# Seven products for eight in the first feed-forward half from the third block on

## The chip, the cores and the metric

The kernel runs on one NeuronCore of one Trainium2 chip. The metric is the device time of one launch in microseconds (us), lower is better. Matrix products run on TensorE (PE), element-wise work on VectorE (DVE) and ScalarE (ACT), a little on GpSimd (POOL), and all DMAs are issued from SyncE's queue (SP).

## The reference, cut to what matters

Batch 8, sequence 576, model width 512; so 4608 tokens. Chunked attention (8 heads of 64, chunks of 64 tokens) gives x; a layer norm and a feed-forward network (FFN) of width 2048 with residual follow; then a gated convolution and a last projection. float32 throughout.

```python
attn = softmax(q_c @ k_c.T / 8) @ v_c              # per chunk and head
xn = (x - mu) / sqrt(var + 1e-6) * g_ln
ch = maximum(xn @ w_ch1, 0) @ w_ch2                # 512 -> 2048 -> 512
x = x + ch
gate = sigmoid(causal_conv5(x, conv_w));  val = x @ w_val
out = (gate * val) @ w_out
```

## The kernel before

The tokens are cut into nine blocks of 512. Activations lie transposed, features on the partitions, tokens along the row. To keep float32 accuracy with the fast matmul type, every operand is split into a high part (rounded to fp32r) and a low part (the rest), and each product is three matmuls: high by high, high by low, low by high.

For each block b, `unit` (four per block, one per 128 tokens) does the attention, the norm and the transposes, and leaves `xn_t[b]` (high and low part) and `X[b]` (the residual). These rooms alternate between two buffers by b % 2. `ffn(b, f)` does one of 16 steps of the FFN: `one` (lines 672 to 674) multiplies the 128 hidden features of step f by four feature groups kk, 4 x 3 matmuls of 512 columns into a PSUM bank h0 or h1; ACT takes hh (relu, high part, line 680), DVE takes hl (low part, line 684); `two` (lines 695 to 697) adds 4 x 3 matmuls of 512 columns into the four PSUM banks y of the block. `residual` (line 705) adds y to X; `conv(b)` does the convolution of the block and stores X and the convolved rows to DRAM. After the last block the gated stage (`prepare`, `val`, `proj`) loads them again.

The weights of the FFN are loaded and split in block 0 (`weights`, `piece`) and stay: W{g}_{i}, g = 0 to 3 for each quarter of the hidden features, i = 0 to 3 for w_ch1 and 4 to 7 for w_ch2, each a room of 128 x 1024 words. When the last block has used them, the rooms take the weights and tiles of the gated stage.

The order of each engine is fixed when the program is built: `Plan` holds operations with an engine, a duration that the author wrote down, dependences and a due time `pri`, and a list scheduler plays them through; each engine's instructions then stand in that order, and wait by semaphores. `when[b, f]` is the due time of a step.

Of the kernel before, what the change touches and what calls it, by code (L numbers as in the profile page):

```python
# [106 lines left out]
def chunk_attention_ffn_gated_conv(  # L107
# [46 lines left out]

    const = ctx.enter_context(tc.tile_pool(name="const", bufs=1))
# [216 lines left out]
    }  # L372
    X, xn_t, xn_ops, X_ops, evict_ops = {}, {}, {}, {}, {}

    def unit(u):
# [178 lines left out]
        xt = f"xn{b % 2}"  # L554
# [13 lines left out]

        def high():
            if o == 0:  # L570
                xn_t[b] = slot(xt, [P, KD, 2, TB, P], F32R, f"xnt{b}")
            nc.scalar.activation(  # L572
                out=xn_t[b][:, :, 0, o],
                in_=st["ps"][:, 1].rearrange("p (f x) -> p f x", x=P),
                func=AF.Copy,
            )

        def low():
            nc.vector.tensor_tensor(  # L579
                out=xn_t[b][:, :, 1, o],  # L580
                in0=st["ps"][:, 1].rearrange("p (f x) -> p f x", x=P),
                in1=xn_t[b][:, :, 0, o].bitcast(F32),
                op=ALU.subtract,
            )
# [30 lines left out]
        eh = op("ACT", 600, high, tn, take(xt) if o == 0 else xn_ops[b][0][0])  # L615
        el = op("DVE", 700, low, eh)
# [38 lines left out]
    nf, yp, y_ops = [0], {}, {}  # L655

    def ffn(b, f):
# [7 lines left out]
        def one(kk):  # L665
            def go():
# [4 lines left out]
                xh, xl = (xn_t[b][:, kk, s].rearrange("p t x -> p (t x)") for s in range(2))  # L671
# [29 lines left out]
        def residual(p):  # L701
            def go():
                for lo, hi, c in parts(b)[1]:
                    x = X[b][:, 2 * p : 2 * p + 2, c : c + hi - lo]
                    nc.vector.tensor_tensor(out=x, in0=yp[b, p][:, :, lo:hi], in1=x, op=ALU.add)

            return go

        xs = [o for both in xn_ops[b] for o in both]
        o1 = None  # L710
        for kk in range(KD):
            o1 = add("PE", 3 * 230.0, one(kk), xs + [w_op[g, kk], o1] + take(ht), pri)
        oh = add("ACT", 620, high, [o1] + take(hht), pri - 1e8)
# [3 lines left out]
        for p in range(2):  # L717
# [5 lines left out]
            if closes:  # L723
                r = add("DVE", 1300, residual(p), [o2[-1]] + X_ops[b] + y_ops.get((b, p), []), pri - 1e8)
# [4 lines left out]
        if b == NBLK - 1:  # L729
            hold(f"W{g}_{KD + f % 4}", *o2)  # L730
            if f % 4 == 3:
                for kk in range(KD):
                    hold(f"W{g}_{kk}", o1)
        if f == KF - 1:
            hold(f"xn{b % 2}", o1)

# [71 lines left out]
    GROUP = 12 * 230.0  # L808
    xg, x2hl, gvhl, wv, wo = {}, {}, {}, {}, {}
# [34 lines left out]
    def val(j, fo):  # L844
# [112 lines left out]
    for b, f in fstep:  # L957
# [3 lines left out]
        ffn(b, f)  # L961
# [55 lines left out]
```

## Time and profile before

| | |
|---|---|
| time, median of 3 runs (lowest to highest) | 1170.92 us (1170.62 to 1171.21) |
| profiled execution, its own time | 1170.97 us |
| span of that execution on the core | 1169.1 us |
| PE busy | 1142.3 us, 98% |
| weight loads (PEld) busy | 909.0 us, 78% |
| DVE busy | 616.2 us, 53% |
| ACT busy | 361.2 us, 31% |
| DMA | 108.67 MB, mean 93 GB/s |

The span is the time from the first to the last instruction of the core; what lies around it is 1.9 us. PE's busy time counts each matmul with its way through the array, so consecutive matmuls overlap and a busy PE says only that one was always under way. PEld are the loads of the stationary operand, which run beside the matmuls. The first 58 us are attention and weights of block 0; the blocks' FFNs run to 964 us, the gated stage to the end.

### The profile page before, as it was taken

What the parts mean: (1) busy time and instruction counts of PE and PEld (TensorE: products, weight loads), DVE (VectorE), ACT (ScalarE), POOL (GpSimd) and SP (SyncE); (2) the same over time, 40 slices, a digit from 0 to 9 for tenths busy, and PEclk for the clock granted to TensorE, in tenths of its full rate; (3) what the DMA queues carried; (4) which work ended last, traced back from release to release, by engine and by line L of the source; (5) the groups of instructions that cost most, each with busy time, mean ns of one, the idle gap of its engine ahead of it and who ended that gap; (6) DMA issues with size and microseconds to landing.
All of it is one profiled execution on the core that took longest, in us unless ns stands there. A gap on an engine that the chain in (4) does not pass through costs nothing.

```text
span 1169.1 us, 17660 instructions
## 1 busy us (share of the span) xinstructions
PE 1142.3 (98%) x7145; PEld 909.0 (78%) x7145; DVE 616.2 (53%) x1058; ACT 361.2 (31%) x625; POOL 26.2 (2%) x78
## 2 busy tenths in 40 slices
PE   5699999999999999999999999999999999999998
PEld 4477887887778788878878877888788877888886
DVE  5889966337354633744563384455337638334321
ACT  5885522212222221222121122221114524434412
POOL 0000000000000000000000000000000000000000
PEclk9789999999999999999999999999999999999999
DMA  8951233122221321222232132223006306434411
GB/s 204 336 191 28 52 103 100 41 51 88 66 73 54 100 50 41 89 66 72 64 91 50 41 98 66 68 67 89 13 1 224 136 1 208 153 127 151 145 46 72
DMA packets 124938, 108.67 MB, mean 93 GB/s; under 512 B 67508, under 2 KB 108472, under 8 KB 124856
## 3 DMA queue, kind: packets, MB, share of 16 engines
q1 hardware_dynamic: 124856, 107.54, 30.9%
q8 instruction: 56, 0.92, 0.3%
q14 instruction: 26, 0.21, 0.1%
HBM read 79.19 MB, written 28.31 MB: 92 GB/s over the span
## 4 chain that ended last, share of the span: by engine, by line
PE 94%; DVE 2%; SPq 1%; DMA 1%; ACT 1%; issue 0%; ACTq 0%; DVEq 0%
PE h L672 12%; PE h L674 12%; PE h L673 12%; PE y L695 12%; PE y L697 11%; PE y L696 11%; PE att L452 4%; PE att L479 3%; PE o L915 3%; PE o L913 3%; PE o L914 3%; PE val L858 3%; PE val L860 3%; PE val L859 3%; PE lo L292 1%; DMA xg<-xgd 1%
## 5 line engine op out<-in xcount | busy, mean ns | idle before, releaser
L672 PE MATMUL h<-xnt,w 128*128 128x512 f32 x576 | 237.0, 411 | 1.4 <-ACT xnt L572 1.4
L684 DVE SCALAR_TENSOR_TENSOR hl<-h,hh 128x512 fp32r<-128x512 f32 x144 | 99.2, 689 | 251.8 <-ACT hh L680 251.8
L695 PE MATMUL y<-hh,w 128*128 128x512 f32 x576 | 231.0, 401 | 0.7 <-ACT hh L680 0.7
L673 PE MATMUL h<-xnt,w 128*128 128x512 f32 x576 | 228.2, 396 | 0.8 <-DVE xnt L579 0.8
L674 PE MATMUL h<-xnt,w 128*128 128x512 f32 x576 | 228.4, 397 | 0.0
L697 PE MATMUL y<-hl,w 128*128 128x512 f32 x576 | 227.4, 395 | 0.0
L696 PE MATMUL y<-hh,w 128*128 128x512 f32 x576 | 226.6, 393 | 0.0
L680 ACT ACTIVATE hh<-h 128x512 fp32r<-128x512 f32 x144 | 86.1, 598 | 436.2 <-PE h L674 430.7
L672 PEld LDWEIGHTS h<-xnt,w 128*128 128x128 f32 x576 | 108.8, 189 | 27.7 <-ACT xnt L572 1.8
L674 PEld LDWEIGHTS h<-xnt,w 128*128 128x128 f32 x576 | 108.8, 189 | 26.0
L697 PEld LDWEIGHTS y<-hl,w 128*128 128x128 f32 x576 | 108.1, 188 | 25.6 <-DVE hl L684 0.4
L695 PEld LDWEIGHTS y<-hh,w 128*128 128x128 f32 x576 | 108.3, 188 | 24.5 <-ACT hh L680 1.1
L673 PEld LDWEIGHTS h<-xnt,w 128*128 128x128 f32 x576 | 109.0, 189 | 23.5 <-DVE xnt L579 1.3
L696 PEld LDWEIGHTS y<-hh,w 128*128 128x128 f32 x576 | 108.3, 188 | 23.5
L777 DVE SCALAR_TENSOR_TENSOR acc<-X,cw_sb,acc 128x516 f32<-128x516 f32 (+1 forms) x144 | 107.4, 751 | 3.3
L864 DVE TENSOR_TENSOR gv<-val,xg 128x512 f32<-128x512 f32 x36 | 24.7, 688 | 70.9 <-PE val L860 70.9
L579 DVE TENSOR_TENSOR xnt<-att,xnt 128x512 fp32r<-128x512 f32 x36 | 24.9, 691 | 66.3 <-ACT X L563 66.3
L858 PE MATMUL val<-x2hl,w 128*128 128x512 f32 x144 | 57.0, 396 | 0.3 <-DVE gv L864 0.3
L860 PE MATMUL val<-x2hl,w 128*128 128x512 f32 x144 | 56.9, 395 | 0.0
L915 PE MATMUL o<-w,gvs 128*128 128x512 f32 x144 | 56.9, 395 | 0.0
L859 PE MATMUL val<-x2hl,w 128*128 128x512 f32 x144 | 56.8, 394 | 0.0
L913 PE MATMUL o<-w,gvs 128*128 128x512 f32 x144 | 56.7, 394 | 0.0
(101 smaller groups left out, 1196.7 us busy)
## 6 DMA issues: line engine op xcount, KB each, us to landing
xg<-xgd SPq DMA_DIRECT2D x36, 512.0 KB, 4.7
raw<-in_moe_w_ch_dram SPq DMA_DIRECT2D x32, 512.0 KB, 8.9
qk_room<-in_q_dram SPq DMA_DIRECT2D x100, 112.0 KB, 2.5
qk_room<-in_k_dram SPq DMA_DIRECT2D x100, 112.0 KB, 2.7
v<-in_v_dram SPq DMA_DIRECT2D x144, 64.0 KB, 2.4
out_dram<-os SPq DMA_DIRECT2D x36, 256.0 KB, 2.0
xgd<-X SPq DMA_DIRECT2D x2, 1024.0 KB, 5.1
xgd<-acc SPq DMA_DIRECT2D x8, 256.0 KB, 2.5
```

The costliest lines, as they stand in the source:

```text
L672: nc.tensor.matmul(ps, wh, xh, start=(kk == 0), stop=False)
L673: nc.tensor.matmul(ps, wh, xl, start=False, stop=False)
L674: nc.tensor.matmul(ps, wl, xh, start=False, stop=(kk == KD - 1))
L684: nc.vector.scalar_tensor_tensor(out=hl, in0=st["ps"], scalar=0.0, in1=st["hh"].bitcast(F32), op0=ALU.max, op1=ALU.subtract)
L695: nc.tensor.matmul(ps, wh[:, s], st["hh"], start=opens, stop=False)
L696: nc.tensor.matmul(ps, wl[:, s], st["hh"], start=False, stop=False)
L697: nc.tensor.matmul(ps, wh[:, s], st["hl"], start=False, stop=closes)
L777: nc.vector.scalar_tensor_tensor(out=a, in0=X[b][:, f, i : i + L], scalar=cw_sb[:, i, f : f + 1], in1=a, op0=ALU.mult, op1=ALU.add,)
L858: nc.tensor.matmul(ps, wh, xh, start=(kk == 0), stop=False)
L859: nc.tensor.matmul(ps, wh, xl, start=False, stop=False)
L860: nc.tensor.matmul(ps, wl, xh, start=False, stop=(kk == KD - 1))
L915: nc.tensor.matmul(ps, al, wh, start=False, stop=(kk == KD - 1))
```

## The change

In blocks 0 and 1 the FFN stays as it was. From block 2 on (`SB = 2`) the first half, hidden = w_ch1.T @ xn, is done per quarter g of the hidden features (512 features by 512 tokens, 512 deep) as a 2 x 2 block product by Strassen's scheme in Winograd's form: seven products of 256 x 256 x 256 in place of eight. Each product is 12 matmuls of 256 columns (two feature groups, two depths, three parts). In detail:

- `weight_sums(g)`, during block 1: forms the four sums of w_ch1's quadrants on DVE (six `whole` steps of two 128x256 adds, four `mix` steps), splits them into high and low parts (ACT, DVE), and stores these and the three plain quadrants to DRAM, 28 pieces `a{g}_{m}` of 512 KB. The rooms W{g}_0 to W{g}_3 are then free.
- Nine of these sixteen rooms become a ring: each product of each block loads its piece from DRAM into the next room of the ring. Six others hold the hidden activations h (three pairs, high and low), one holds an operand.
- `unit` leaves the normalised activations of these blocks unsplit (`xs`); `operands(b)` forms on DVE the four sums of their quadrants and splits the seven operands. They live in block 1's and block 0's former rooms and in W3_3 (`late_tile`).
- `hidden(b, g)`: products 2, 1, 6, 5, 3, 7, 4 in two PSUM banks that are reused within the group. ACT copies of a bank (`shot`) and DVE additions (`join`, `last_join`) make the four quadrants of the hidden activations; relu and split follow as before; the second half is 48 matmuls of 512 columns as before.
- Rooms of the gated stage move, because the ring holds theirs longer. The due times take 21 x 234 ns a step from block 2 on.

The diff, cut to its core:

```diff
+    SB = 2
...
-        t_end += 24 * 230.0
-    ends = {b: when[b, KF - 1] + 24 * 230.0 for b in range(NBLK)}
+        t_end += 24 * 230.0 if b < SB else 21 * 234.0
...
+    ROOMS = [f"W{g}_{i}" for g in range(NG) for i in range(KD)]
+    RING, PAIRS = ROOMS[:9], [ROOMS[9 + 2 * i : 11 + 2 * i] for i in range(3)]
+
+    def late_tile(i):
+        if i not in late:
+            tag, n = ((f"xn{SB % 2}b", 2), (f"xn{1 - SB % 2}a", KD), ("W3_3", 1))[i]
+            late[i] = slot(tag, [P, n, 2 * DM], F32R, f"late{i}")
+        return late[i]
...
+            eh = el = op("ACT", 600, plain, tn, xn_room)
...
+    def weight_sums(g):
...
+        def keep(m, mh, kh):
+            def go():
+                for i in range(2):
+                    for s, t in enumerate(part(mh, 2 * kh + i)):
+                        nc.sync.dma_start(out=a_dram[g, m][:, s, i].bitcast(F32), in_=t)
+
+            a_store[g, m] = add("SP", 2000, go, ready, pri + 5000.0)
+            reads.append(a_store[g, m])
...
+        def whole(ut, m, kh):
+            def go():
+                us[ut] = slot(ut, [P, XW], F32, f"as{g}_{m}{kh}")[:, : 4 * P].rearrange("p (k x) -> p k x", k=2)
+                for i in range(2):
+                    hi, lo = part(m, 2 * kh + i)
+                    nc.vector.tensor_tensor(out=us[ut][:, i], in0=hi, in1=lo, op=ALU.add)
+
+            o = add("DVE", 840, go, ready + take(ut), pri)
...
+        def split(m, ut, i, dep):
+            rt = f"o{'21'[i]}"
...
+            oh = add("ACT", 620, high, [dep] + take(rt), pri)
+            ol = add("DVE", 700, low, [oh], pri)
+            a_store[g, m] = add("SP", 1300, store, [ol], pri)
+            hold(rt, a_store[g, m])
...
+        a = whole("u0", 1, 0)
+        b = whole("u1", 1, 1)
+        s1 = mix("u0", "u0", "u1", ALU.add, a, b)
+        l1 = split("5", "u0", 0, s1)
+        hold("u1", s1)
+        c = whole("u1", 0, 0)
+        s2 = mix("u1", "u0", "u1", ALU.subtract, s1, c)
...
+            hold(f"W{g}_{kk}", last_use[g, kk], *reads)
...
+    def operands(b):
...
+        s2 = split("2", q21, *done)
+        s1 = split("1", q11, *done)
+        t1 = mix(q11, q12, q11, s1)
+        s3 = split("3", q22, *done)
+        t3 = mix(q12, q22, q12, t1)
+        t2 = mix(q22, q22, q11, s3, t3)
+        t4 = mix(q21, q22, q21, s2, t2)
+        last = [split("6", q22, t2, t4), split("5", q11, t1, t2), split("7", q12, t3), split("4", q21, t4)]
+        hold("xs", *last)
...
+        def product(m, into, new, deps):
+            rt = RING[ring_n[0] % len(RING)]
+            ring_n[0] += 1
...
+                x = operand(m)
+                for f in range(2):
+                    for kk in range(2):
+                        wh, wl = (w[m][:, s, kk, f * P : (f + 1) * P] for s in range(2))
+                        for i, (l, r) in enumerate(((wh, 0), (wh, 1), (wl, 0))):
+                            nc.tensor.matmul(
+                                st[into][:, f],
+                                l,
+                                x[:, r, kk],
+                                start=new and f == kk == i == 0,
+                                stop=kk == 1 and i == 2,
+                                skip_group_check=True,
...
+            at = pri + 1400.0 * MS.index(m)
+            ld = add("SP", 1300, load, [a_store[g, m]] + take(rt), at - 16000.0)
+            o = add("PE", 12 * 119.0, go, [ld, B_op[b, m]] + deps, at)
+            hold(rt, o)
...
+        m2 = product("2", "b", True, take(tb))
+        m1 = product("1", "a", True, take(ta))
+        s1 = shot("a", "hh0", m1)
+        c11 = join("hh0", "b", ALU.add, s1, m2)
+        m6 = product("6", "a", False, [m1, s1])
+        m5 = product("5", "b", True, [c11])
+        u2 = shot("a", "hh1", m6)
+        s5 = shot("b", "hl0", m5)
+        m3 = product("3", "b", False, [m5, s5])
+        m7 = product("7", "a", False, [m6, u2])
+        c12 = join("hh1", "b", ALU.add, u2, m3)
+        u3 = shot("a", "hl1", m7)
+        hold(ta, u3)
+        c22 = join("hl0", "hl1", ALU.add, s5, u3)
+        m4 = product("4", "b", True, [c12])
...
+        c21 = add("DVE", 700, last_join, [c22, m4], pri - 1e7)
+        hold(tb, c21)
+
+        hs, h_ops = {}, {}
+        for p, half, tag, dep in ((0, 0, "hh0", c11), (0, 1, "hh1", c12), (1, 1, "hl0", c22), (1, 0, "hl1", c21)):
...
+    XG = [f"W{g}_{i}" for g, lo in ((0, 0), (2, KD)) for i in range(lo, lo + KD)]
+    X2 = [f"W{g}_{i}" for g in (1, 2) for i in range(KD)]
```

The order that the scheduler makes of it, at three places. First TensorE in the middle of block 2. Before, a first-half step (h from xnt and the weights w) and a second-half step (y from hh and hl) of 12 matmuls each alternate:

```order
L695 MATMUL y_1_0_2623<-hh_1_2655,w_520 128x512
L696 MATMUL y_1_0_2623<-hh_1_2655,w_520 128x512
L697 MATMUL y_1_0_2623<-hl_1_2665,w_520 128x512
L695 MATMUL y_1_0_2623<-hh_1_2655,w_520 128x512
L696 MATMUL y_1_0_2623<-hh_1_2655,w_520 128x512
L697 MATMUL y_1_0_2623<-hl_1_2665,w_520 128x512
L452 MATMUL att_2637<-ident,p_2674 128x128 x4
L672 MATMUL h_2_2657<-xnt_1952,w_403 128x512
L673 MATMUL h_2_2657<-xnt_1952,w_403 128x512
L674 MATMUL h_2_2657<-xnt_1952,w_403 128x512
L672 MATMUL h_3_2703<-xnt_1952,w_169 128x512
```

Now products of 256 columns (m from an operand `late` and a loaded piece a) stand between halves of second-half steps; att are the attention's matmuls:

```order
L1044 MATMUL yB_3076<-h_1_1_3281,w_844 128x512
L950 MATMUL m_2_2_3435<-late_2810,a_2_5_3122 128x256 x12
L503 MATMUL att_3448<-kT_3287,qT_3270 64x64 x16
L1042 MATMUL yA_3059<-h_1_1_3280,w_872 128x512
L1043 MATMUL yA_3059<-h_1_1_3280,w_872 128x512
L1044 MATMUL yA_3059<-h_1_1_3281,w_872 128x512
L1042 MATMUL yA_3059<-h_1_1_3280,w_872 128x512
L1043 MATMUL yA_3059<-h_1_1_3280,w_872 128x512
L1044 MATMUL yA_3059<-h_1_1_3281,w_872 128x512
L950 MATMUL m_2_2_3435<-late_2810,a_2_3_3154 128x256 x12
L476 MATMUL att_3448<-ident,p_3472 128x128 x4
```

Each product follows on 6 to 12 matmuls of the second half or on attention work; the number of second-half matmuls has not changed. Second, TensorE at the border of blocks 1 and 2. Before, the first h of block 2 stands ahead of block 1's last y:

```order
L672 MATMUL h_0_2558<-xnt_1952,w_325 128x512
L673 MATMUL h_0_2558<-xnt_1952,w_325 128x512
L674 MATMUL h_0_2558<-xnt_1952,w_325 128x512
L695 MATMUL y_0_0_1760<-hh_15_2562,w_1581 128x512
L696 MATMUL y_0_0_1760<-hh_15_2562,w_1581 128x512
L697 MATMUL y_0_0_1760<-hl_15_2567,w_1581 128x512
L695 MATMUL y_0_0_1760<-hh_15_2562,w_1581 128x512
L696 MATMUL y_0_0_1760<-hh_15_2562,w_1581 128x512
L697 MATMUL y_0_0_1760<-hl_15_2567,w_1581 128x512
L695 MATMUL y_1_0_1771<-hh_15_2562,w_1581 128x512
L696 MATMUL y_1_0_1771<-hh_15_2562,w_1581 128x512
L697 MATMUL y_1_0_1771<-hl_15_2567,w_1581 128x512
```

Now the products of block 2, all but the first, stand behind block 1's last y, one behind the other:

```order
L747 MATMUL y_1_0_1856<-hh_15_2807,w_1666 128x512
L748 MATMUL y_1_0_1856<-hh_15_2807,w_1666 128x512
L749 MATMUL y_1_0_1856<-hl_15_2812,w_1666 128x512
L476 MATMUL att_2790<-ident,p_2829 128x128 x4
L503 MATMUL att_2790<-v_2775,p_2829 64x65 x16
L950 MATMUL m_2_0_2894<-late_2068,a_0_1_2186 128x256 x12
L950 MATMUL m_2_0_2894<-late_2810,a_0_6_2211 128x256 x12
L950 MATMUL m_2_0_2944<-late_2810,a_0_5_2222 128x256 x12
L950 MATMUL m_2_0_2894<-late_2810,a_0_7_2319 128x256 x12
L950 MATMUL m_2_0_2944<-late_2810,a_0_3_2302 128x256 x12
L950 MATMUL m_2_1_3009<-late_2068,a_1_2_2405 128x256 x12
L950 MATMUL m_2_0_3031<-late_2919,a_0_4_2372 128x256 x12
```

What stood on both sides of the border is now on one side. Third, DVE in block 1, from one low part of hidden activations (hl_2) to the next (hl_3 and hl_4). Before:

```order
L684 SCALAR_TENSOR_TENSOR hl_2_1879<-h_2_1822,hh_2_1865 128x512
L777 SCALAR_TENSOR_TENSOR acc_3_1844<-X_389,cw_sb,acc_3_1844 128x512 x3
L524 TENSOR_SCALAR rs_1900<-att_1781 128x8
L525 RECIPROCAL rs_1900<-rs_1900 128x8
L527 TENSOR_TENSOR x_1903<-att_1781,rs_1900 128x2x4x64
L535 BN_STATS stat_1905<-x_1903 128x6
L537 BN_AGGR mv_1906<-stat_1905 128x2
L538 TENSOR_SCALAR ve_1908<-mv_1906 128x1
L684 SCALAR_TENSOR_TENSOR hl_3_1929<-h_3_1867,hh_3_1922 128x512
L546 TENSOR_SCALAR xn_1934<-x_1903,mv_1906,rstd_1924 128x512
L579 TENSOR_TENSOR xnt_1952<-att_1781,xnt_1952 128x4x128
L684 SCALAR_TENSOR_TENSOR hl_4_1993<-h_4_1918,hh_4_1987 128x512
```

Now with the sums of weights (as):

```order
L736 SCALAR_TENSOR_TENSOR hl_2_1964<-h_2_1907,hh_2_1950 128x512
L1098 SCALAR_TENSOR_TENSOR acc_3_1929<-X_419,cw_sb,acc_3_1929 128x512 x3
L823 TENSOR_TENSOR as_10_1985<-w_197 128x256
L823 TENSOR_TENSOR as_10_1985<-w_248 128x256
L548 TENSOR_SCALAR rs_1991<-att_1866 128x8
L549 RECIPROCAL rs_1991<-rs_1991 128x8
L551 TENSOR_TENSOR x_1994<-att_1866,rs_1991 128x2x4x64
L559 BN_STATS stat_1996<-x_1994 128x6
L561 BN_AGGR mv_1997<-stat_1996 128x2
L562 TENSOR_SCALAR ve_1999<-mv_1997 128x1
L736 SCALAR_TENSOR_TENSOR hl_3_2015<-h_3_1952,hh_3_2010 128x512
L570 TENSOR_SCALAR xn_2025<-x_1994,mv_1997,rstd_2017 128x512
```

Sums stand between hl_2 and hl_3; behind hl_4 the next sums follow at once.

## Rows read from the trace of the kernel before

**Rows 1.** The page: engines; granted TensorE clock in 40 slices; chain that ended last.

```profile
PE 1142.3 (98%) x7145; PEld 909.0 (78%) x7145; DVE 616.2 (53%) x1058; ACT 361.2 (31%) x625; POOL 26.2 (2%) x78
...
PEclk9789999999999999999999999999999999999999
...
PE 94%; DVE 2%; SPq 1%; DMA 1%; ACT 1%; issue 0%; ACTq 0%; DVEq 0%
```

**Rows 2.** Windows: 0 to 100 us, the gated stage, then blocks 1 and 2.

```profile
core 0: us, PE busy (x) PEld busy (x) DVE busy (x) ACT busy (x) POOL busy (x), PEclk, DMA share, GB/s
0.00:100.00 100.00, 78.01 (x594) 56.34 (x595) 78.76 (x156) 70.64 (x128) 5.16 (x17) 0.90 0.72 214
...
1000.00:1100.00 100.00, 100.00 (x432) 80.78 (x431) 34.96 (x54) 39.12 (x69) 0.00 (x0) 1.00 0.43 138
...
166.30:264.50 98.20, 98.20 (x677) 78.56 (x676) 48.65 (x83) 20.80 (x35) 2.64 (x8) 1.00 0.25 71
264.50:365.50 101.00, 101.00 (x689) 80.82 (x689) 50.92 (x86) 21.46 (x37) 2.64 (x8) 1.00 0.25 68
```

**Rows 3.** Groups by line and shape on TensorE: second half, transposes, loads (mean ns).

```profile
L674 PE MATMUL h<-xnt,w 128*128 128x512 f32 x576 | 228.4, 397 | 0.0
...
L674 PEld LDWEIGHTS h<-xnt,w 128*128 128x128 f32 x576 | 108.8, 189 | 26.0
...
L452 PE MATMUL att<-ident,p 128*128 128x128 f32 x144 | 22.2, 277 | 1.6 <-ACT p L508 1.6
...
L452 PEld LDWEIGHTS att<-ident,p 128*128 128x128 f32 x144 | 17.9, 141 | 6.3 <-ACT p L508 1.9
```

**Rows 4.** Timeline of TensorE about 502 us: start, duration, engine, line.

```profile
502.02 0.39 PE L697 MATMUL y<-hl,w 128*128 128x512 f32 x1
...
502.26 0.60 PE L452 MATMUL att<-ident,p 128*128 128x128 f32 x4
502.58 0.19 PEld L672 LDWEIGHTS h<-xnt,w 128*128 128x128 f32 x1
502.61 0.48 PE L672 MATMUL h<-xnt,w 128*128 128x512 f32 x1
502.69 0.19 PEld L673 LDWEIGHTS h<-xnt,w 128*128 128x128 f32 x1
502.93 0.40 PE L673 MATMUL h<-xnt,w 128*128 128x512 f32 x1
```

**Rows 5.** Groups by line and shape on DVE and ACT (mean ns).

```profile
L684 DVE SCALAR_TENSOR_TENSOR hl<-h,hh 128x512 fp32r<-128x512 f32 x144 | 99.2, 689 | 251.8 <-ACT hh L680 251.8
L680 ACT ACTIVATE hh<-h 128x512 fp32r<-128x512 f32 x144 | 86.1, 598 | 436.2 <-PE h L674 430.7 <-DVE X L705 4.9
...
L427 DVE STREAM_TRANSPOSE qT<-qk_room 128x512 f32<-128x512 f32 x28 | 30.8, 1101 | 0.0
...
L500 DVE TENSOR_TENSOR p<-att,mx 128x512 f32<-128x512 f32 x36 | 24.9, 692 | 1.2
...
L579 DVE TENSOR_TENSOR xnt<-att,xnt 128x512 fp32r<-128x512 f32 x36 | 24.9, 691 | 66.3 <-ACT X L563 66.3
...
L499 DVE TENSOR_REDUCE mx<-att 128x8 f32<-128x512 f32 x36 | 24.6, 683 | 4.2 <-PE att L479 4.1
...
L572 ACT ACTIVATE xnt<-att 128x512 fp32r<-128x512 f32 x36 | 21.5, 597 | 68.2 <-PE att L452 68.1
...
L705 DVE TENSOR_TENSOR X<-y,X 128x896 f32<-128x896 f32 x4 | 4.3, 1086 | 2.3 <-PE y L697 2.2
...
L563 ACT ACTIVATE X<-att 128x256 f32<-128x256 f32 x8 | 2.6, 386 | 0.0
...
L705 DVE TENSOR_TENSOR X<-y,X 128x256 f32<-128x256 f32 x4 | 1.7, 420 | 2.2 <-PE y L697 2.1
...
L705 DVE TENSOR_TENSOR X<-y,X 128x128 f32<-128x128 f32 x4 | 1.1, 287 | 2.3 <-PE y L697 2.2
```

**Rows 6.** DMA issues by line: count, KB each, median us to landing.

```profile
xg<-xgd SPq DMA_DIRECT2D x36, 512.0 KB, 4.7
raw<-in_moe_w_ch_dram SPq DMA_DIRECT2D x32, 512.0 KB, 8.9
```

More of the change, by code (lines that the diff above doesn't have):

```diff
@@ L653, in weights, with residual @@
         )
-    nf, yp, y_ops = [0], {}, {}
+    nf, yp, y_ops, last_use = [0], {}, {}, {}
+    def residual(b, p):
+        def go():
+            for lo, hi, c in parts(b)[1]:
+                x = X[b][:, 2 * p : 2 * p + 2, c : c + hi - lo]
+                nc.vector.tensor_tensor(out=x, in0=yp[b, p][:, :, lo:hi], in1=x, op=ALU.add)
+        return go
     def ffn(b, f):
@@ L723, in ffn @@
             if closes:
[L724 removed]
+                r = add("DVE", 1300, residual(b, p), [o2[-1]] + X_ops[b] + y_ops.get((b, p), []), pri - 1e8)
                 y_ops[b, p] = [r]
@@ L728, in ffn @@
         hold(hlt, *o2)
[L729 to L733, printed above, removed]
         if f == KF - 1:
             hold(f"xn{b % 2}", o1)
+    MS = ("2", "1", "6", "5", "3", "7", "4")
+    WA = dict(zip(MS, ("12", "11", "S2", "S1", "S4", "S3", "22")))
+    a_dram = {
+        (g, m): dram.tile([P, 2, 2, 2 * P], F32R, name=f"a{g}_{m}") for g in range(NG) for m in MS
+    }
@@ new lines, in chunk_attention_ffn_gated_conv, with quadrant, mix, go @@
+    B_op = {}
+    def operands(b):
+        pri = when[b, 0] - 12000.0
+        done = [o for both in xn_ops[b] for o in both]
+        if b == SB:
+            for m in "6537":
+                hold(f"o{m}", *take(f"xn{1 - SB % 2}"))
+            hold("o4", *take("W3_3"))
+        def quadrant(kh, h):
+            return xn_t[b][:, 2 * kh : 2 * kh + 2, h * 2 * P : (h + 1) * 2 * P]
+        def mix(to, x, y, *deps):
+            def go():
+                nc.vector.tensor_tensor(out=quadrant(*to), in0=quadrant(*x), in1=quadrant(*y), op=ALU.subtract)
+            return add("DVE", 700, go, deps, pri)
+        def split(m, src, *deps):
+            def high():
+                nc.scalar.activation(out=operand(m)[:, 0], in_=quadrant(*src), func=AF.Copy)
+            def low():
+                t = operand(m)
+                nc.vector.tensor_tensor(
+                    out=t[:, 1], in0=quadrant(*src), in1=t[:, 0].bitcast(F32), op=ALU.subtract
+                )
+            oh = add("ACT", 620, high, list(deps) + take(f"o{m}"), pri)
+            B_op[b, m] = ol = add("DVE", 700, low, [oh], pri)
+            return ol
+        q11, q12, q21, q22 = ((kh, h) for kh in range(2) for h in range(2))
+        s2 = split("2", q21, *done)
[7 more added lines that the diff above has]
+        hold("xs", *last)
@@ L960, in chunk_attention_ffn_gated_conv @@
                 unit(u)
-        ffn(b, f)
+            if b >= SB:
+                operands(b)
+        if b < SB:
+            ffn(b, f)
+            if b == SB - 1 and f % 4 == 3:
+                weight_sums(f // 4)
+        elif f % 4 == 0:
+            hidden(b, f // 4)
         if (b, f) == (0, KF // 2 + 1):
```

200 lines of the change are left out of this document (170 added, 30 removed).

## Prediction

> **What bounds the kernel now.** I read the page first: TensorE (PE) is busy for 98% of the span and holds 94% of the chain of work that ended last, at the higher clock level (2.4 GHz) after the first slices [rows 1]. Then the windows: in blocks 1 and 2 PE is busy for the whole of each window, VectorE (DVE) for 48.65 of 98.20 us and 50.92 of 101.00 us, ScalarE (ACT) for a fifth [rows 2]. So between about 100 and 960 us the time is the number of PE instructions times their interval. Busy durations don't give that interval, since matmuls overlap (a mean of 397 ns [rows 3]); a window that holds nothing but 512-column matmuls does: 432 of them fill 100.00 us [rows 2], which is **231.5 ns each**. The weight loads go beside them, one per matmul, 189 ns long and pipelined [rows 3, 4].
>
> **The change, part by part.**
>
> *PE, first half of blocks 2 to 8.* A block loses 16 x 4 x 3 = 192 matmuls of 512 columns and gets 4 groups x 7 products x 12 = 336 of 256 columns; for seven blocks 1344 go and 2352 come. What goes is worth 1344 x 0.2315 = 311.1 us. What comes depends on an interval that this trace does not show, that of a 256-column matmul with its own weights. I bound it:
> - From below: 110 ns. After four transposes the load for L672 starts at 502.58 and that for L673 at 502.69, while L673's matmul follows at 502.93 [rows 4]; so the array was ready to stream L672 within 110 ns of its load's start. 2352 x 0.110 = 258.7 us.
> - From above: the transposes of 128 columns, each with its load. Four take 0.60 us and one takes 277 ns, so they are (600 - 277) / 3 = 108 ns apart [rows 3, 4]. A straight line through (128, 108) and (512, 231.5) gives 149 ns at 256. That is 2352 x 0.149 = 350.4 us, more than what goes.
> - Between them, half of the 512-column interval: 115.8 ns, 272.4 us.
> The line from above mixes two kinds of instruction: a transpose's load takes 141 ns and that of the FFN's matmuls 189 ns [rows 3]. The nearest row is the 512-column matmul itself, so I start from its half and allow a fixed part of some 6 ns per instruction: **119 ns**, 2352 x 0.119 = 279.9 us. The gain is 311.1 - 279.9 = **31.2 us**, 4.5 us a block.
>
> The Trainium skill ("TensorE: Matmul & The Clock Gate", "Back-to-back issue gap") puts the warm gap at columns / 2.4 + 2.5 ns: 215.8 ns for 512 and 109.2 for 256. The trace disagrees for 512 columns by 16 ns (231.5), so here each matmul, or each column, pays something that the rule leaves out. The same page's "LDWEIGHTS" gives 107 ns for 128 columns, which fits within the 110 ns above. By the rule's 109.2 ns the sum would be 2352 x 0.1092 = 256.8 us and the gain 54.3; this is a rival below.
>
> *Handshakes in the steady groups.* Seven products share two PSUM banks, and each next use of a bank waits for an ACT copy or a DVE join. In the order some six matmuls of the second half (6 x 0.2315 = 1.39 us) or an attention step lie between most products. The tightest pair, product 1 then 6 on one bank, needs one ACT copy of 128x512 (0.60 us [rows 5]) plus hops; 5 after 1 needs a copy and a join (0.60 + 0.69) against a product (1.43) and two such fillings. A queue delay of one or two DVE jobs of 0.7 us fits. I take 0 for these; if the cover failed by 0.3 us at each of 196 products it would be 59 us.
>
> *DVE and ACT in those blocks.* Per block DVE gets 16 joins of 0.69 us and, for the operands, 11 jobs instead of 4: 11.0 + 4.8 = 15.9 us on 50.9 [rows 2, 5], about 67 of 96. ACT gets 16 copies of 0.60 us and some 3 more: 11.4 us on 21.5. Neither bounds.
>
> *DMA.* 196 loads of 512 KB in seven blocks: 28 x 0.524 = 14.7 MB a block, 152 GB/s on 68 GB/s. The first 100 us carried 214 GB/s at a share of 0.72 [rows 2], with loads of this size landing in 8.9 us; later ones land in 4.7 us [rows 6]. A room is free when the product nine places back is done; nine places are some 31 us (96.5 / 28 x 9), so even 9 us are covered three times over. SP's queue is in order, and the loads stand in it among the attention's loads and the convolution's stores, which wait for DVE; a delay of a few us there is covered too. 0 us; without that cover each us late at every product would be 196 us.
>
> *Block 1: sums of weights.* Four groups, each 12 DVE jobs of 128x256 (0.42 us, the nearest row is L705's of that shape) and 8 of 128x512 (0.69): 4 x 10.6 = 42.2 us. With block 1's 48.65, and the operands of block 2 (11 x 0.69, of which 4 were there): 95.7 of 98.2 us. DVE goes from half to nearly full, and the hl of the FFN (L684, now L736), for which PE waits, is queued behind these sums and behind the stream transposes (1.1 us). PE has one step in hand: 12 matmuls (2.8 us) against 0.60 + 0.69 and hops, so some 1.3 us of delay is hidden, one or two jobs. I take **2 us** of PE idle; 16 steps late by one job each would be 11.
>
> *From block 1 to block 2.* Before, PE ran block 2's first matmuls between the last ones of block 1. Now four of the seven operands lie in the room of block 1's own activations, free only after its last first-half matmul (time 0 here), and six products stand in a row on PE without filling. By the order and rows 5: PE has scores, one product and the 12 last matmuls until 4.6 us, then waits for the softmax and its copy until about 6. DVE meanwhile does hl (until 1.6), an operand (2.2), the softmax (1.4), two stream transposes (2.2) and the residual (two of 1.09 + 0.29), and reaches product 1's low part only at about 9.3: PE waits some 3 us. Four mixes and the next split (2.8 + 1.4) hold product 6 until 13.5: another 2.8. Then a join late, some 1 to 2. Sum **8 us**, once; 3 if DVE overlaps better, 12 if the loads for those transposes come late. At the later block borders each operand's room is free a product or more earlier and 18 matmuls lie between: 0.
>
> *Rest.* Block 0's activations are split in two rooms: a 128x256 copy is 386 ns, two are 0.17 us more than one of 597 [rows 5]; 0.3 us at the start. The gated stage has its 864 matmuls as before; its first pieces go to rooms that the last products free before 48 matmuls of the second half (11 us) are done. 0 us.
>
> **Sum** against the profiled execution, 1170.97 us (span 1169.1; the median of the runs is 1170.92, the same): 1170.97 - 31.2 + 2 + 8 + 0.3 = **1150 us**.
>
> **Rivals.**
> 1. *Products as fast as their loads*: interval 110 to 115.8 ns, gain 52.4 to 38.7. For it: PE was ready 110 ns after a load's start. Against: at 512 columns something is paid on top, and a load that starts only when the matmul before begins to stream leaves no slack. 1129 to 1142 us. By the skill's gap it would be 1127.
> 2. *The short matmul pays the transposes' fixed part*: 149 ns, 39 us more than what goes, with the 10.3 us of waits **1221 us**, slower. It decides from (311.1 - 10.3) / 2352 = 128 ns on; at that interval all that the eighth product saves goes into the second set of weight loads. For it: one matmul more per weight load is what the scheme costs, 2352 loads where there were 1344. Against: the ready time of 110 ns.
> 3. *The waits are larger*: DVE late in block 1 at most steps (11 us) and at the border (12), and a few at the joins: 15 more than I took, 1165 us; with 125 ns besides, 1179.
>
> **How the numbers follow.** Forecast (116 to 125 ns, 5 to 15 us of waits: 1142 to 1168): 0.58. Rival 1: 0.20. Rival 2: 0.11. Rival 3: 0.11, half of it above 1168. The range reaches from 1130, which leaves out the lower end of rival 1, to 1172, which leaves out rival 2 and the end of rival 3. A measurement here tells 0.2%, 2.3 us, from no change. Faster: 0.58 + 0.20 + 0.04 = 0.82; same 0.05; slower 0.13.
>
> **What the profile after would show.** The products' interval: twelve matmuls in a stretch without waits take 1.43 us if I am right, 1.32 by rival 1, 1.79 by rival 2. Blocks 3 to 7 stand about 96.5 us apart where they stood 101. PE's idle time lies around the border of blocks 1 and 2, some 8 us, released by DVE, and a little in block 1, where DVE is busy above 90%. If instead PE waits for ring loads (DMA) or for joins all through blocks 2 to 8, the zeros above were wrong; if block 1 is longer by 10 us, its sums were undersized.

## The result and the profile after

| | before | after |
|---|---|---|
| time, median of 4 runs each | 1170.77 us | 1144.76 us |
| ratio, 95% interval | | 0.978 (0.9763 to 0.9797) |
| profiled execution's own time / span | 1170.97 / 1169.1 us | 1143.88 / 1142.1 us |
| PE busy; DVE; ACT | 98%; 53%; 31% | 97%; 66%; 40% |
| DMA | 108.67 MB | 226.32 MB |

The kernel is 26 us faster; forecast were 21, and the range holds the time. First the page of after: engines, the granted clock in 40 slices, the chain that ended last, and the loads of the ring (count, KB, median us to landing).

```profile
PE 1108.6 (97%) x8153; PEld 940.6 (82%) x8153; DVE 750.5 (66%) x1303; ACT 462.3 (40%) x806; POOL 31.9 (3%) x78
...
PEclk9989999998999999999999999999999999999999
...
PE 91%; DVE 3%; SPq 2%; DMA 2%; ACT 1%; issue 0%; DVEq 0%; ACTq 0%
...
a<-a SPq DMA_DIRECT2D x196, 512.0 KB, 4.2
```

PE is still the bound; one slice of PEclk in the FFN, the tenth, dropped below 9 (a dip that before didn't have there [rows 1]). A ring load lands in 4.2 us though DMA moves twice as much.

The windows (us, busy time and count of each engine, granted clock, DMA share, GB/s): block 1 up to 260 us, then blocks 3 and 4, each cut from its first product to the next block's.

```profile
core 0: us, PE busy (x) PEld busy (x) DVE busy (x) ACT busy (x) POOL busy (x), PEclk, DMA share, GB/s
...
166.70:260.00 93.30, 93.30 (x652) 74.44 (x651) 80.62 (x155) 28.27 (x48) 3.19 (x7) 1.00 0.61 196
...
364.80:460.90 96.10, 96.10 (x833) 85.35 (x832) 64.89 (x111) 34.49 (x59) 3.64 (x8) 1.00 0.77 224
460.90:557.10 96.20, 96.20 (x834) 85.33 (x833) 63.66 (x109) 34.56 (x60) 3.64 (x8) 1.00 0.70 222
```

A block with products takes 96.1 or 96.2 us; blocks 3 to 7 all do. Before, it was 101.0 [rows 2]. DVE is at 80.62 of 93.30 us in block 1, and PE busy throughout: the sums of weights cost it nothing there. In blocks 3 and 4 DVE is at 64.9 and 63.7 us, about two thirds.

What a product costs stands in the timeline of PE in block 3 (start, duration, engine, line):

```profile
400.07 1.58 PE L950 MATMUL m<-late,a 128*128 128x256 f32 x12
401.48 0.39 PE L1042 MATMUL yB<-h,w 128*128 128x512 f32 x1
```

From the first of a product's twelve matmuls to the start of what follows: 401.48 - 400.07 = 1.41 us, **118 ns each** (the median over all of the kernel's consecutive product matmuls is 118 too). So a block saves 192 x 0.2315 - 336 x 0.118 = 4.80 us, and the windows show 101.0 - 96.15 = 4.85. The 196 products' handshakes (the copies and joins that free their PSUM banks) and ring loads cost nearly nothing: all waits of product matmuls in blocks 3 to 8 (364 to 938 us) that the view lists are

```profile
PE m L950 <- ACT c_hl L970: 0.4, 1, 0.4
```

Seven blocks at 4.80 make 33.6 us; the profiled spans differ by 27.0. The missing 6.6 us, and 1.6 us more that other places gave back, are at **the border of blocks 1 and 2**, where the timeline shows DVE, ACT, SP's queue and PE (in brackets: idle before, and who ended it):

```profile
259.85 5.17 SPq L439 DMA_DIRECT2D qk_room<-in_k_dram  x8
...
262.63 0.69 DVE L845 TENSOR_TENSOR late<-as,late 128x512 fp32r<-128x512 f32 x1 [0.70 <-ACT late L841]
...
265.12 0.37 SPq L848 DMA_DIRECT2D a<-late  x1
...
266.56 1.71 PE L950 MATMUL m<-late,a 128*128 128x256 f32 x12 [0.79 <-DVE hl L736]
...
268.35 1.11 DVE L451 STREAM_TRANSPOSE qT<-qk_room 128x512 f32<-128x512 f32 x1
...
269.00 0.61 ACT L902 ACTIVATE late<-xs 128x512 fp32r<-128x512 f32 x1
...
269.31 1.06 DVE L451 STREAM_TRANSPOSE kT<-qk_room 128x512 f32<-128x512 f32 x1
...
270.22 2.46 DVE L702 TENSOR_TENSOR X<-y,X 128x128 f32<-128x128 f32 x4
...
272.61 0.67 DVE L906 TENSOR_TENSOR late<-xs,late 128x512 fp32r<-128x512 f32 x1
...
272.88 2.02 PE L950 MATMUL m<-late,a 128*128 128x256 f32 x12
273.31 2.87 DVE L896 TENSOR_TENSOR xs<-xs 128x512 f32<-128x512 f32 x4
...
274.76 1.15 ACT L902 ACTIVATE late<-xs 128x512 fp32r<-128x512 f32 x2 [1.37 <-DVE xs L896]
...
276.96 0.54 PE L950 MATMUL m<-late,a 128*128 128x256 f32 x1 [2.06 <-ACT late L902]
...
278.03 4.21 PE L950 MATMUL m<-late,a 128*128 128x256 f32 x18 [0.53 <-DVE late L906]
```

The last sum of weights is done on DVE at 263.3 (262.63 + 0.69). Its store stands on SP behind eight loads of attention rows and is issued at 265.12; the DMA view of that moment gives its landing 2.9 us later, at about 268.0:

```profile
a<-late SPq DMA_DIRECT2D x1, 512.0 KB, 2.9
```

Only then may ACT write operand 1 into the same room. It does so at 269.00, and DVE, in order behind two stream transposes and the residual, writes the low part at 272.61. So most of the time between landing and low part, 4.6 us, is DVE's order. The plan put the transposes and the residual ahead of the low part; in the run below in which the last sums have other rooms, the low part stands ahead of the residual. The room thus acts mainly through the order that is made with it, less through a wait while the kernel runs.

Product 1 stands behind the attention step that PE starts at 272.26, begins at 272.88 and loses 0.3 us on the low part. The four mixes follow (273.31, 2.87 us), and product 6 starts only at 276.96 and stalls again until 278.03. Two other waits don't hang on operand 1: product 2 waits 0.8 us at 266.56 for block 1's last hl, and the attention step at 272.26 waits 0.8 us, until ACT has copied the softmax's rows. Adding up how far matmul starts here lie behind their usual intervals gives 5.7 us (to some 0.5 us, since the usual intervals vary too).

The rest is the clock. Windows just behind:

```profile
276.00:280.00 4.00, 2.51 (x10) 2.21 (x11) 3.97 (x9) 2.04 (x4) 0.00 (x0) 0.63 1.01 280
280.00:284.00 4.00, 4.00 (x21) 4.00 (x21) 3.24 (x7) 1.19 (x2) 0.93 (x1) 0.52 0.37 134
284.00:290.00 6.00, 6.00 (x54) 6.00 (x52) 3.70 (x7) 1.86 (x3) 0.00 (x0) 1.00 0.77 246
```

The clock stood at its lower level, 1.2 GHz, from 277.0 to 283.9 us, after the stalls; 26 product matmuls were then 213 ns apart instead of 118, 2.5 us more. 5.7 + 2.5 = 8.2 us at the border. Of the 1.6 us given back, 0.9 are the gated stage's, which took 204.5 us (937.6 to 1142.1) where before took 205.4 (963.7 to 1169.1); 0.7 are a wait of before's PE for ACT at the end of its FFN (at 960 us), which is gone; the start gave nothing (the first FFN matmul comes at 57.9 us instead of 57.8).

### The profile page after: what moved, and what is told of

Same layout as the page of the kernel before. It is cut to its first block, busy times and chain, and to the rows that moved or that the text cites. A ratio compares the mean times of both kernels' runs of the same rounds, so it can differ in the third digit from the quotient of the medians.

```text
span 1142.1 us, 20763 instructions
## 1 busy us (share of the span) xinstructions
PE 1108.6 (97%) x8153; PEld 940.6 (82%) x8153; DVE 750.5 (66%) x1303; ACT 462.3 (40%) x806; POOL 31.9 (3%) x78
## 2 busy tenths in 40 slices
DMA packets 162393, 226.32 MB, mean 198 GB/s; under 512 B 71668, under 2 KB 118776, under 8 KB 162296
## 4 chain that ended last, share of the span: by engine, by line
PE 91%; DVE 3%; SPq 2%; DMA 2%; ACT 1%; issue 0%; DVEq 0%; ACTq 0%
PE m L950 24%; PE yA L1042 5%; PE yB L1042 5%; PE yB L1043 4%; PE yB L1044 4%; PE yA L1043 4%; PE yA L1044 4%; PE att L476 4%; PE att L503 3%; PE val L1181 3%; PE val L1182 3%; PE o L1237 3%; PE val L1183 3%; PE o L1238 3%; PE o L1236 3%; PE h L724 3%
## 5 line engine op out<-in xcount | busy, mean ns | idle before, releaser
L950 PEld LDWEIGHTS m<-late,a 128*128 128x128 f32 x2352 | 302.8, 190 | 19.0 <-ACT late L902 2.3
L950 PE MATMUL m<-late,a 128*128 128x256 f32 x2352 | 313.4, 284 | 3.9 <-ACT late L902 2.1
L977 DVE TENSOR_TENSOR c_hh<-c_hh,m 128x512 f32<-128x512 f32 x56 | 38.4, 686 | 101.7 <-ACT c_hh L970 65.1
L1042 PE MATMUL yA<-h,w 128*128 128x512 f32 x224 | 92.0, 411 | 0.0
L1042 PE MATMUL yB<-h,w 128*128 128x512 f32 x224 | 90.4, 404 | 0.0
L1043 PE MATMUL yB<-h,w 128*128 128x512 f32 x224 | 88.3, 394 | 0.0
L1043 PE MATMUL yA<-h,w 128*128 128x512 f32 x224 | 88.3, 394 | 0.0
L1044 PE MATMUL yA<-h,w 128*128 128x512 f32 x224 | 88.3, 394 | 0.0
L1044 PE MATMUL yB<-h,w 128*128 128x512 f32 x224 | 88.2, 394 | 0.0
L970 ACT ACTIVATE c_hh<-m 128x512 f32<-128x512 f32 x56 | 33.5, 598 | 108.6 <-PE m L950 108.6
L1012 ACT ACTIVATE h<-c_hh 128x512 fp32r<-128x512 f32 x56 | 35.4, 632 | 84.7 <-DVE c_hh L977 84.4
L970 ACT ACTIVATE c_hl<-m 128x512 f32<-128x512 f32 x56 | 33.5, 598 | 80.6 <-PE m L950 80.6
L1238 PE MATMUL o<-w,gvs 128*128 128x512 f32 x144 | 56.8, 394 | 0.0
L1237 PE MATMUL o<-w,gvs 128*128 128x512 f32 x144 | 56.8, 394 | 0.0
L1236 PE MATMUL o<-w,gvs 128*128 128x512 f32 x144 | 56.7, 394 | 0.0
L724 PE MATMUL h<-xnt,w 128*128 128x512 f32 x128 | 53.4, 417 | 1.2 <-ACT xnt L606 1.2
L725 PE MATMUL h<-xnt,w 128*128 128x512 f32 x128 | 51.8, 404 | 0.7 <-DVE xnt L610 0.7
```

The source lines that it names most:

```text
L724: nc.tensor.matmul(ps, wh, xh, start=(kk == 0), stop=False)
L950: nc.tensor.matmul(st[into][:, f], l, x[:, r, kk], start=new and f == kk == i == 0, stop=kk == 1 and i == 2, skip_group_check=True,)
L1042: nc.tensor.matmul(ps, wh, hh, start=opens and f == 0, stop=False)
L1043: nc.tensor.matmul(ps, wl, hh, start=False, stop=False)
L1044: nc.tensor.matmul(ps, wh, hl, start=False, stop=closes and f == 3)
L1236: nc.tensor.matmul(ps, ah, wh, start=(kk == 0), stop=False)
```

## Experiments

My theory was: the gain is the products' instruction time and nothing else; ring, joins and sums are covered; what is missing went at the border, through rooms and DVE's order there. "Changed kernel" below is the kernel after, and its time is the 1144.76 us above; each ratio is to the kernel before, measured beside that run.

**The price of a short matmul by itself.** In the kernel before, the first half of blocks 2 to 8 in pieces of 256 or 128 columns:

```diff
+                if b < 2:
...
+                    return
+                for n in range(2):
+                    for i, (l, r) in enumerate(((wh, xh), (wh, xl), (wl, xh))):
+                        nc.tensor.matmul(
+                            ps[:, n * 256 : (n + 1) * 256],
+                            l,
+                            r[:, n * 256 : (n + 1) * 256],
...
```

For b < 2 the three matmuls stay as they were; the second run has `range(4)` and 128 in place of `range(2)` and 256.

> The kernel before, with each of the 1344 first-half matmuls of 512 columns in blocks 2 to 8 cut into two of 256 columns, each with its own weight load; nothing else differs. It prices the short matmul by itself. Theory (what the products pay, 118 ns, is the price of any 256-column matmul of this type): two take 236 ns where one took 231.5, so 1344 x 4.5 ns = 6 us more, about 1177 us. Rival (the line through the transposes, 149 ns): 1344 x 66 ns = 89 us more, about 1260 us. Rival (118 ns holds only where new weights and operands come with it, here it is half of 231.5): no change, 1171 us.

1175.84 us, ratio 1.0043 (1.0023 to 1.0064): 5.0 us more by the ratio. The timeline shows twelve in 405.70 - 404.09 = 1.61 us, of which some 0.2 (1.61 - 12 x 0.118) go with the changes of kind at either end, from transposes and to attention; the median of all 2537 consecutive pairs is 118 ns.

```profile
404.09 1.67 PE L679 MATMUL h<-xnt,w 128*128 128x256 f32 x12
405.70 0.51 PE L479 MATMUL att<-v,p 64*64 64x65 f32 x19
```

So 118 ns is the price of a 256-column matmul with its own load in the old kernel as in the new one, and half of 231.5 (115.8) is nearly reached. The line through the transposes falls, and so does no change at all.

> The same with four matmuls of 128 columns. Theory A (a fixed part of 4.5 ns and 0.443 ns a column, the line through 118 at 256 and 231.5 at 512): 61 ns each, 245 for four, 18 us more, about 1189 us. Theory B (below 256 columns the weight load takes over, since a load was never seen to follow another in less than 108 to 110 ns): 4 x 109 = 436 ns, 1344 x 204 ns = 275 us more, about 1446 us. I hold B likelier.

1456.38 us, one run. 48 matmuls of 128 columns take 411.05 - 405.74 = 5.31 us, 111 ns each, hardly less than one of 256:

```profile
405.74 5.47 PE L679 MATMUL h<-xnt,w 128*128 128x128 f32 x48
411.05 0.44 PE L707 MATMUL y<-hh,w 128*128 128x512 f32 x1
```

Theory B's number: from 512 to 256 columns the interval falls by 113 ns, from 256 to 128 by 7 only, to about that of the transposes before (108 ns, worked out from [rows 3, 4]). That it is the weight load which sets this floor is argued from there; no run here takes the load away. 256 columns is the shortest piece among these that still runs at about its columns' pace. A scheme that halves the blocks once more, with 49 products of 128 columns for 64, would by this price lose all: 588 matmuls of 111 ns a block are 65 us against 44.4 (an estimate).

**The ring.** Three rooms in place of nine:

```diff
-    RING, PAIRS = ROOMS[:9], ...
+    RING, PAIRS = ROOMS[:3], ...
```

> The changed kernel with a ring of three rooms in place of nine; a load can be issued when the product three places back is done, so two places of 3.43 us, 6.9 us, lie between that and its use. Theory (nine rooms cover the loads several times over; a piece lands 4.2 us after its issue): still covered, 1145 to 1150 us. Rival (the queue of SP or the busier DMA engines make the loads late by several us, so that nine rooms are needed): 2 us or more at each of 196 products, 1500 us or more.

1146.44 us (1145.59 and 1147.29), ratio 0.9789 (0.9744 to 0.9834): the same within its interval, which with two runs is 5 us to either side. PE's waits of product matmuls from 290 to 940 us begin to name the load:

```profile
PE m L950 <- DMA a<-a: 2.1, 3, 1.1
PE m L950 <- DVE acc L1098: 0.8, 1, 0.8
```

3 waits of at most 1.1 us: two places ahead, 6.9 us (2 x 96.1 / 28), just cover a landing of 4.3 us in the median. Three rooms nearly do; that left rooms for the runs below.

**DVE's room in block 1.** Each of the 48 small adds done twice:

```diff
                 for i in range(2):
-                    hi, lo = part(m, 2 * kh + i)
-                    nc.vector.tensor_tensor(out=us[ut][:, i], in0=hi, in1=lo, op=ALU.add)
+                    for _ in range(2):
+                        hi, lo = part(m, 2 * kh + i)
+                        nc.vector.tensor_tensor(out=us[ut][:, i], in0=hi, in1=lo, op=ALU.add)
```

> The changed kernel with each of the 48 adds of 128x256 in the weight sums done twice, 20.2 us more on DVE in block 1, where DVE was busy for 80.6 of 93.3 us. Theory (DVE in block 1 has 13 us of room, then it bounds): 7 to 10 us longer, about 1153 us. Rival 1 (the queue already delays PE for every job): the whole 20 us, 1165 us. Rival 2 (the scheduler moves the sums behind what PE needs, and block 2 hides them): under 2 us, 1146 us.

1156.3 us (1154.38 and 1158.21), ratio 0.9873 (0.9816 to 0.993): 11.5 more than the changed kernel, a little over the theory's 7 to 10, which lies within the interval (some 7 us to either side). The window over block 1 and the border, then PE's waits there:

```profile
166.00:280.00 114.00, 103.75 (x718) 79.78 (x716) 105.00 (x209) 31.57 (x54) 3.30 (x8) 1.00 0.54 174
```

```profile
PE y L749 <- DVE hl L736: 3.5, 5, 1.6
PE att L476 <- ACT p L532: 1.9, 2, 1.1
PE att L503 <- DVE kT L451: 1.6, 1, 1.6
```

DVE is busy for 105 of 114 us and PE waits for hl, the softmax and the transposes. So of the 20.2 us added some 9 were hidden, give or take the interval: block 1 had about that much of DVE's time to spare, and the sums are free there only up to that.

**Which block starts.**

```diff
-    SB = 2
+    SB = 3        # 1 in the second run
```

> The changed kernel with the products from the fourth block on: six blocks in place of seven, the sums formed in block 2. Theory (each block gains 4.8 us, 192 x 231.5 ns less 336 x 118 ns, and the border costs its 7 to 8 us once, wherever it lies): 4.8 us more, 1149.6 us. Rival (part of the gain or loss depends on block 1 with its sums, or the gain is larger in some blocks): differs by over 2 us from that.

1144.27 us, ratio 0.9784 (0.9765 to 0.9803): not 4.8 us slower, but the same. A block less of products costs 4.8 us, so something else gave as much. The blocks with products stand 96.0 to 96.2 us apart as in the changed kernel; the border is what differs. SP's queue, operand 1's low part and the window at it:

```profile
361.38 0.34 SPq L848 DMA_DIRECT2D a<-late  x1
361.84 2.64 SPq L467 DMA_DIRECT2D v<-in_v_dram  x4
...
369.07 0.68 DVE L906 TENSOR_TENSOR late<-xs,late 128x512 fp32r<-128x512 f32 x1
```

```profile
360.00:380.00 20.00, 17.48 (x166) 15.09 (x165) 15.13 (x27) 10.54 (x20) 0.11 (x1) 1.00 0.65 198
```

The last sum's store is issued at 361.38, and product 2 starts at 367.3: the store has 5.9 us, where in the changed kernel it had 1.4 (265.12 to 266.56). Operand 1's low part follows 1.8 us after product 2's start (369.07), there 6.1 us after it (272.61). PE loses 3.1 us there by the same count of late starts and the clock stays at 1.00. 5.7 + 2.5 - 3.1 = 5.1 us given back, which is the block's 4.8. The theory's "7 to 8 us, wherever it lies" fell. That the border's price goes by how long before it the last sum is stored fits these rows, but this run moves the sums into another block with them, so it doesn't show it by itself.

> The products from the second block on: eight blocks. Theory as for the fourth block: 4.8 us less, 1140 us, if block 0 can take the sums. Rival: DVE is busy for 92 of 109 us in block 0, the sums bring 42 us; so DVE bounds there and block 0 ends 20 to 25 us later: 1160 to 1165 us.

1173.49 us, ratio 1.0025 (1.0013 to 1.0037): slower than before. Block 0, where DVE splits all weights, can't take the sums:

```profile
58.00:170.00 112.00, 102.92 (x695) 81.34 (x693) 102.46 (x202) 62.96 (x111) 2.85 (x7) 0.94 0.56 184
```

```profile
PE att L476 <- DVE xn L570: 9.7, 1, 9.7
PE y L747 <- ACT w L279: 7.9, 1, 7.9
```

The rival's direction, by more than its 20 to 25 us: block 0 ends 30 us later (its residual starts at 195.5 us, in the changed kernel at 165.5). The waits that the view lists for PE between 160 and 220 us sum to 29 us, and for 41 us between 165.7 and 213.5 the clock stood at its lower level.

**The border.** First DVE's order alone: the operands of block 2 due first.

```diff
-        pri = when[b, 0] - 12000.0
+        pri = when[b, 0] - (1e7 if b == SB else 12000.0)
```

> The changed kernel with the operands of block 2 ahead of everything else on DVE and ACT (due time earlier). At the border PE lost about 5 us in waits and 2.5 us at the lower clock. Theory (DVE's order at the border, transposes and residual ahead of the operands, holds the products): 3 to 5 us less, 1140 to 1142 us. Rival (the rooms of block 1's activations hold them, free too late whatever DVE's order): within 1 us of 1145.

1144.36 us, ratio 0.9785 (0.9768 to 0.9801), the waits of PE at the border 2.1, 0.8, 0.8 and 0.5 us as in the changed kernel. But this run tested neither theory nor rival. The traces have every engine's instructions in the same order as the changed kernel (8153 on PE, 1303 on DVE, 806 on ACT, every line and tile alike): it is that kernel once more, and says only that its time repeats within 0.4 us. So the due time was not what placed the operands. The likely reason is that the scheduler already placed each as soon as it was ready in its plan, but no run shows the plan.

Then rooms: five for the ring, four own ones for operands 6, 5, 3, 7, and the attention of block 2 earlier; the due time stays as in the run before.

```diff
-    RING, PAIRS = ROOMS[:9], ...
+    RING, OWN, PAIRS = ROOMS[:5], dict(zip("6537", ROOMS[5:9])), ...
...
+        if m in OWN:
...
+                late[m] = slot(OWN[m], [P, 2 * DM], F32R, f"late_{m}")
...
-            pri = qk_pri = v_pri = when[b, 0] - LEAD_TILE + STEP_TILE * o
+            pri = qk_pri = v_pri = when[b, 0] - LEAD_TILE + STEP_TILE * o - (14000.0 if b == SB else 0.0)
```

> A ring of five rooms; four operands get rooms of their own, which the ring gave up, so that none waits for block 1's activations; operands first on DVE as in the run with their due time earlier, and the attention of block 2 begins 14 us earlier. Theory (the border costs 7 to 8 us through those rooms and the order): most of it returns, 1138 to 1140 us. Rival (products in a row without filling are held by their own copies and joins): 2 us at most, 1143 us.

1147.19 us, ratio 0.981 (0.9793 to 0.9827): nothing gained. The timeline has SP's store, then DVE and ACT on operands; PE's waits and the window follow:

```profile
266.44 0.37 SPq L852 DMA_DIRECT2D a<-late  x1
...
274.89 0.68 DVE L910 TENSOR_TENSOR late<-xs,late 128x512 fp32r<-128x512 f32 x1
...
277.06 0.63 ACT L906 ACTIVATE late<-xs 128x512 fp32r<-128x512 f32 x1 [2.27 <-DVE xs L900]
```

```profile
PE att L480 <- ACT p L536: 2.7, 1, 2.7
PE m L954 <- DVE c_hh L983: 1.5, 1, 1.5
```

```profile
266.00:280.00 14.00, 9.35 (x104) 7.84 (x102) 9.85 (x15) 4.80 (x9) 0.00 (x0) 0.79 0.68 198
```

The store of the last sum is still issued at 266.44, operand 1's low part comes at 274.89, and the mixes and operand 6 behind it. PE itself waits longest for the softmax (2.7 us) and for the join of products in a row (1.5 us), and the clock fell to its lower level from 274.2 to 284.5 us. So the four rooms, the due time and the lead together are not enough. What is left as a suspect is the room in which sums are put together, which operand 1 takes over; my theory had not separated it from the four.

So the sums of groups 1 to 3 went into two rooms of the ring, which now takes these two last:

```diff
-    RING, OWN, PAIRS = ROOMS[:5], ...
+    RING, OWN, PAIRS = [ROOMS[i] for i in (0, 1, 4, 2, 3)], ...
...
-            rt = f"o{'21'[i]}"
+            rt = f"o{'21'[i]}" if g == 0 else ROOMS[2 + i]
```

> As in the run with rooms of their own and an earlier attention, but with the attention of block 2 where it was, and with the sums of the later three groups put together in two other rooms (of the five of the ring, free then), so that operands 1 and 2 of block 2 don't wait for the last sum's store. In the changed kernel the store of that sum is issued at 265.1 us, behind eight loads on SP's queue, and operand 1's low part comes at 272.6. Theory (that room is what holds the border): 4 to 7 us less than the changed kernel, 1138 to 1141 us, and no stretch at the lower clock. Rival (the copies and joins of products without filling hold it): within 1.5 us of 1145.

1141.15 us, ratio 0.9752 (0.9733 to 0.977): 3.6 us less than the changed kernel, in the theory's direction, just outside its 1138 to 1141 us. The two ratios' intervals overlap slightly (the changed kernel's is 0.9763 to 0.9797); the border's rows tell the two apart better than the times.

```profile
PE m L958 <- ACT c_hh L980: 0.7, 1, 0.7
PE m L958 <- ACT c_hl L980: 0.7, 1, 0.7
```

```profile
166.00:266.00 100.00, 100.00 (x686) 79.99 (x685) 85.09 (x161) 31.34 (x53) 3.31 (x8) 1.00 0.51 170
266.00:286.00 20.00, 18.57 (x180) 16.66 (x179) 19.06 (x32) 10.70 (x19) 0.00 (x0) 1.00 0.90 298
```

PE's longest waits at the border are 0.7 us, and now for the products' own copies, which were the rival's hold; the clock stays at 1.00. By late starts the border costs 2.1 us instead of 8.2. That the whole shows 3.6 and not 6 has two parts in the trace: the first FFN matmul comes at 59.9 us instead of 57.9 (it varies from 57.1 to 60.1 between the runs), and in the last block PE waits 1.2 us for copies instead of 0.4.

> The same with the attention of block 2 starting 14 us earlier, so that its activations are there before the border; by the order the products then stand between block 1's last matmuls. Theory: 1 to 2 us less than without, 1137 to 1139 us. Rival (the earlier attention pushes more work of DVE into block 1, and PE waits there): 2 us or more than without.

1139.29 us, ratio 0.9738 (0.9716 to 0.9761). The theory's size, but the two intervals overlap, so it can't be told from the run without the lead; it is below the changed kernel's, 0.978 (0.9763 to 0.9797), by intervals that don't touch. It also differs from the run with rooms of their own (1147.19 us) in nothing but the rooms of the sums and the order of the ring, and is 7.9 us faster, with the clock at its higher level throughout the border: this pair shows that, with the four rooms and the lead in place, the room of the sums is what held the border. Whether it alone, without the four rooms, would have been enough, no run tells. PE's waits at the border:

```profile
PE m L958 <- DVE c_hh L987: 0.9, 1, 0.9
PE att L507 <- issue: 0.8, 1, 0.8
```

> The same with 8 us in place of 14: between the two, about 1139 us, if the border's waits shrink with the lead; the lowest of the three if DVE in block 1 is what limits the lead.

1144.32 us, ratio 0.9776 (0.9754 to 0.9798). Not between the two: 4.5 us of late starts at the border, 3.4 us at the lower clock (282.0 to 285.4), and in the last block PE waits 3.2 us for copies where it waits 1.0 with the 14 us. The border's waits are of a new kind:

```profile
PE m L958 <- DMA a<-a: 4.0, 2, 2.6
```

Two products wait for their ring loads, which neither of the two other runs shows. By the landings these are the loads issued at 270.90 and 278.12, 3.7 us before the products start (274.63 and 281.78): they were issued late, and landed no later than others. A due time of 6 us more or less puts the engines in another order, and the list scheduler's order isn't monotonic in it. Why the order issues these loads so late I did not follow up.

The lowest time is that with the 14 us: 1139.3 us, 31.6 below the kernel before, measured beside it (1170.85).

## Why the prediction was right, step by step

- *The price of the products* was the step that all hung on. 119 ns was forecast, 118 measured; 311.1 - 2352 x 0.118 = 33.6 us against 31.2. The choice of the nearest row (half of the 512-column interval and a little) was right, the line through the transposes was not: 128 columns cost 111 ns as well, but as a floor, not as a fixed part. Rival 2 dies with the run of 256 columns.
- *Rival 1* (110 to 115.8 ns) did not come. The products stood 213 ns apart at 1.2 GHz and 118 at 2.4 GHz, 11 ns more than half of 213: twice the clock doesn't buy twice the pace, and 110 ns is reached by 128 columns only (111). The Trainium skill ("TensorE: Matmul & The Clock Gate", "Back-to-back issue gap") gives the isolated matmul columns / 1.2 at the lower level and columns / 2.4 + 2.5 ns at the higher, 213.3 and 109.2 ns for 256 columns: the trace agrees at the lower one (213) and not at the higher (118). The prediction left out that the section speaks of the isolated matmul.
- *Handshakes and the ring at zero*: right. One wait of 0.4 us in blocks 3 to 8 of those listed; ring loads land in 4.2 us in the median, faster than the 4.7 to 8.9 us of the rows I went by, and even a ring of three changes nothing that can be told.
- *Block 1*: 2 us forecast, none measured. DVE was at 86% there, not 97%: most of block 2's operands, which I had put into it, fell behind the border. That it was near the edge is shown by the doubled adds (11.5 us).
- *The border*: 8 us forecast, 5.7 us of waits and 2.5 us of lower clock measured. That the sum is right is luck: the waits were smaller, and the clock, which I had not named, made up for it. The order of events came as worked out: operand 1's low part was done 8.3 us after block 1's last first-half matmul (273.3 against 265.0; forecast 9.3), then came the mixes, and product 6 started 12.0 us after it (277.0; forecast 13.5). But before product 1 PE waited 1.1 us instead of 3, and I put the hold down to block 1's rooms and DVE's queue. The pair of runs with and without other rooms for the sums shows that it was the room of the last sum; DVE's order, made by the plan with that room, carried most of it. The store's place on SP's queue (1.8 us from sum to issue) belongs to the same chain, but no run moved it alone.
- *The rest*: 0.3 us for the split room in block 0 can't be told from the 1 to 2 us by which the first 60 us vary.

One sum of the prediction doesn't come out: with 116 ns and 5 us of waits the time is 1170.97 - 38.3 + 5 = 1138 us, not the 1142 at which it lets its own case begin; the upper end, 1168, does.

Summed anew with 118 ns, no idle in block 1 and 8.2 at the border: 1170.97 - 33.6 + 8.2 + 0.3 = 1145.9 us, against 1143.9 of the profiled execution. The prediction's 1150 was 6 us above that: 2.4 from the products, 2 from block 1, the rest from what the gated stage and other places gave back.

## What to carry to other kernels

Before a scheme with fewer but shorter instructions is written, price the shorter instruction in the old kernel by cutting the old one: one run tells whether its interval shrinks with its length or stands on a floor, here 118 ns at 256 columns and 111 at 128. Work put into a block in which an engine was half idle was free here until its last result had to be stored and its room handed on; follow that one store and room. And when an edit of due times changes nothing, compare the engines' orders first: if they are the same, nothing was tested, and the cause still has to be found.

## What the hardware showed that I had not expected

- Two levels of the same instruction: 256 columns are 118 ns apart at 2.4 GHz and 213 ns at 1.2 GHz. At the lower clock a product takes 1.8 times as long.
- Stalls of 2.1 and 0.5 us with short matmuls between them, after 0.8 and 0.8 shortly before, were followed by a stretch of 6.9 us at the lower clock (277.0 to 283.9), and the border in the run that starts with block 3, with 3.1 us of late starts in all, was not.
